# RMS weight moved into the PSUM eviction of the first two blocks, and a re-ordered start, in a fused sliding-window attention and SwiGLU kernel

## The chip, the cores and the metric

One core of one Trainium2 chip runs the whole program. The metric is the device time of one execution in microseconds, measured on the chip. A time is the median of several executions.

I write TensorE, VectorE, ScalarE and GpSimd for what the profile calls PE, DVE, ACT and POOL. PEld is TensorE's loading of weights, which overlaps its matmuls. SP is the queue that issues the stores.

## The reference

```python
def _attn_ref(q, k, v, n_sink, window):          # 4 batches, 8 heads, 768 positions, 64 wide
    scores = 1/sqrt(D) * q @ k^T
    keep = (key position < n_sink) | (0 <= query - key < window)     # n_sink 4, window 128
    a = softmax(where(keep, scores, -1e9))
    return a @ v

def _moe_ref(x, w_gate, w_val, w_out, rms_g):    # 3072 tokens, 512 wide, 1536 inner
    xn = x / sqrt(mean(x*x) + 1e-6) * rms_g
    g = xn @ w_gate
    return (g * sigmoid(g) * (xn @ w_val)) @ w_out
```

The attention output, with heads side by side, is the x of the second part.

## The kernel before

The 3072 tokens are 24 blocks of 128. Four blocks make a group of 512 tokens for the feed-forward part. A prologue runs the attention of blocks 0 and 1. Then the feed-forward matmuls of group 0 start on those two blocks (`fa`), while blocks 2 and 3 are still in attention. From there on, units of attention ("slots") are woven between parts of the feed-forward matmuls.

The unit names recur below. `unit_t1` and `unit_t` transpose q and k of a block. `unit_bias`, `unit_sp` and `unit_s` make scores and exponentials. `unit_av` multiplies by v. `unit_rms` and `unit_xr` normalise. `unit_x` transposes the normalised block, so that it can be the moving operand of the gate and val matmuls.

The normalisation multiplies by the weight `gb` on VectorE, and ScalarE copies the transposed block out of PSUM:

```python
    def unit_xr(g):
        ...
            nc.vector.scalar_tensor_tensor(
                out=XR[g][-1], in0=x16[:, c], scalar=y[:, 4:5], in1=gb[:, c],
                op0=ALU.mult, op1=ALU.mult,
            )
    def unit_x(g):
        ...
            nc.scalar.copy(
                out=XNT[G][:, c.start // P:c.stop // P, tb * P:(tb + 1) * P],
                in_=ps[:, 0:n].rearrange("p (k c) -> p k c", c=P),
            )
```

The end of the prologue, and the slots of group 0 (cut):

```python
        unit_warm(WARM[1])                   # filler matmuls
        unit_x(0)
        unit_t1(2, 0)
        unit_warm(WARM[2])
        unit_x(1)
        ...
        pools.close()                        # the prologue's PSUM pool ends here
    ...
        slots = [[lambda: unit_t1(5, 0)], [lambda: unit_t1(5, 1)], [lambda: unit_s(4)],
                 [lambda: unit_sink_scores(0, 4)], [lambda: unit_t(6)], []]
        for g in range(5, NB + 3):
            slots += step(g)
```

`weave` spreads the slots of a group evenly over its parts, so the number of slots decides which part comes ahead of which unit.

The softmax here doesn't subtract the row's maximum and nothing guards it: scores larger than these inputs give would overflow.

## Time and profile before

| | before |
|---|---|
| time, median of 3 executions | 255.21 us (254.88 to 255.5) |
| span of the profiled execution | 252.6 us |
| TensorE busy | 238.8 us, 95% |
| first gate matmul starts | 16.90 us |
| k of block 8 lands | 51.61 us |
| first gate matmul of group 1 | 73.35 us |

These are lines of the profile page. In the slices each digit is a busy share in tenths, and one slice is 6.3 us.

```profile
span 252.6 us, 4804 instructions
PE 238.8 (95%) x1733; PEld 127.4 (50%) x1760; DVE 181.1 (72%) x474; ACT 139.6 (55%) x312; POOL 98.1 (39%) x129
...
PE   5988979989999999999999999999999999999994
...
PEclk9999999999999999999999999999999999999999
DMA  9999999999999999650120550321321013200022
```

The lost time of TensorE is at the start. The view by windows says how much. Its columns are the window, its length, then the busy us of PE, PEld, DVE, ACT and POOL with the number of instructions, and last the granted clock, the DMA share and GB/s.

```profile
0.00:17.00 17.00, 12.50 (x102) 5.83 (x104) 11.00 (x46) 9.16 (x21) 15.70 (x26) 1.00 1.54 151
17.00:40.00 23.00, 20.47 (x234) 16.27 (x233) 16.39 (x43) 15.63 (x35) 17.63 (x22) 1.00 1.96 175
40.00:60.00 20.00, 18.51 (x199) 12.84 (x199) 17.76 (x50) 15.78 (x35) 13.82 (x17) 1.00 1.98 174
60.00:100.00 40.00, 39.68 (x309) 21.06 (x314) 35.52 (x100) 28.83 (x67) 27.49 (x33) 1.00 2.38 163
```

The waits of TensorE are in its timeline (start, duration, line, operation, count, and in brackets the idle time ahead of it with what ended it). L581 is the helper of the gate and val matmuls, L563 transposes a normalised block, L251 transposes q and k.

```profile
16.90 1.03 PE L581 MATMUL pg<-xnt,wg 128*128 128x256 bf16 x8 [0.46 <-ACT xnt L567]
...
50.68 0.40 PE L251 MATMUL pqk<-ident,qs 128*128 128x128 bf16 x4 [0.61 <-DMA qs<-in_q_dram]
51.65 0.40 PE L251 MATMUL pqk<-ident,ks 128*128 128x128 bf16 x4 [0.58 <-DMA ks<-in_k_dram]
51.89 1.03 PE L581 MATMUL pvl<-xnt,wv 128*128 128x512 bf16 x4
```

The last pair before 52 us are the transposes of block 8. They wait for its q and k. The chain of waits (start, duration, what) agrees: it reaches back from TensorE's work to this load.

```profile
39.14 12.47 DMA ks<-in_k_dram
51.61 0.04 issue
51.65 0.40 PE pqk L251 x4
52.05 0.86 PE pvl L581 x4
...
59.74 0.86 PE po L622 x4
60.60 0.44 PE pss L321 x4
```

The load was issued at 39.14 us and landed 12.47 us later, behind everything issued before it. From the transposes of block 8 to the first gate matmul of group 1 (51.65 to 73.35 us), the pieces of this chain add up to 15.87 us of TensorE, 4.16 of VectorE and 1.47 of ScalarE.

### The profile page before, as it was taken

The numbers are of one execution on the slowest core, as the hardware profiler recorded it, in microseconds if no ns is written. First come the engines' busy times: TensorE is split into PE (matmuls) and PEld (weight loads), VectorE is DVE, ScalarE is ACT, GpSimd is POOL, SyncE is SP. The second block draws the span as 40 slices with busy tenths as digits, with TensorE's granted clock in tenths as the row PEclk, the third lists the DMA queues.
The fourth block names the chain that finished last, engine by engine and source line by source line (L and its number), as shares of the span: only waits on it lengthen the run. The fifth ranks groups of instructions, "written<-read, shape, count | busy, mean of one in ns | idle before, by whom it ended". The sixth has DMA issues, their size and how long they took to land.

```text
span 252.6 us, 4804 instructions
## 1 busy us (share of the span) xinstructions
PE 238.8 (95%) x1733; PEld 127.4 (50%) x1760; DVE 181.1 (72%) x474; ACT 139.6 (55%) x312; POOL 98.1 (39%) x129
## 2 busy tenths in 40 slices
PE   5988979989999999999999999999999999999994
PEld 1446858655555454454454454454454544444441
DVE  5666869889779999539989459988359991287700
ACT  2757858879886465556473546466545441323211
POOL 8996779289985763134041004044201000000000
PEclk9999999999999999999999999999999999999999
DMA  9999999999999999650120550321321013200022
GB/s 130 152 174 189 189 156 188 182 155 150 194 186 161 155 131 155 128 168 13 21 56 10 145 145 3 64 58 19 113 84 23 0 21 98 91 0 0 0 86 83
DMA packets 105850, 25.74 MB, mean 102 GB/s; under 512 B 95074, under 2 KB 102754, under 8 KB 105827
## 3 DMA queue, kind: packets, MB, share of 16 engines
q0 software_dynamic: 80704, 13.90, 76.5%
q1 hardware_dynamic: 24082, 11.28, 18.6%
q10 hardware_dynamic: 1040, 0.26, 0.5%
q8 instruction: 14, 0.23, 0.4%
q14 instruction: 10, 0.07, 0.1%
HBM read 28.31 MB, written 6.29 MB: 137 GB/s over the span
## 4 chain that ended last, share of the span: by engine, by line
PE 67%; DMA 12%; DVE 8%; POOL 7%; ACT 2%; issue 2%; POOLq 0%; ACTq 0%; DVEq 0%
PE po L622 23%; PE pvl L581 18%; PE pg L581 18%; DMA wv<-in_moe_w_val_dram 7%; DMA ks<-in_k_dram 5%; PE pT L413 3%; DVE p L599 2%; POOL v L124 2%; POOL qs L111 2%; DVE hT L607 2%; PE pv L456 1%; PE pv L452 1%; PE pv L444 1%; POOL ks L111 1%; ACT et L422 1%
## 5 line engine op out<-in xcount | busy, mean ns | idle before, releaser
L581 PE MATMUL pg<-xnt,wg 128*128 128x512 bf16 (+1 forms) x317 | 73.5, 352 | 1.1 <-ACT xnt L567 0.5
L581 PE MATMUL pvl<-xnt,wv 128*128 128x512 bf16 (+1 forms) x322 | 73.4, 353 | 0.4
L622 PE MATMUL po<-wo,hT 128*128 128x512 bf16 x279 | 64.9, 379 | 0.5 <-issue 0.2
L594 ACT ACTIVATE th<-pg 128x512 bf16<-128x512 f32 x72 | 42.9, 596 | 39.1 <-PE pg L581 39.0
L599 DVE SCALAR_TENSOR_TENSOR p<-th,pg 128x512 bf16<-128x512 bf16 x72 | 48.9, 679 | 20.1 <-ACT th L594 19.5
L607 DVE TENSOR_TENSOR hT<-p,pvl 128x512 bf16<-128x512 bf16 x72 | 49.2, 684 | 3.7 <-PE pg L581 0.5
L581 PEld LDWEIGHTS <-wv 128*128 128x128 bf16 x328 | 30.5, 98 | 27.2 <-issue 1.1
L581 PEld LDWEIGHTS <-wg 128*128 128x128 bf16 x328 | 30.4, 98 | 26.9 <-issue 1.2
L422 ACT ACTIVATE et<-pT 128x512 bf16<-128x512 f32 x76 | 39.8, 602 | 4.8 <-PE pT L413 4.6
L390 POOL TENSOR_SCALAR_AFFINE_SELECT et<-et 128x512 bf16<-128x512 bf16 x20 | 13.1, 660 | 73.9 <-ACT et L422 73.9
L622 PEld LDWEIGHTS <-hT 128*128 128x128 bf16 x288 | 26.7, 98 | 29.7 <-issue 0.8
L494 ACT ACTIVATE sq<-x 128x256 bf16<-128x256 bf16 x48 | 20.0, 417 | 26.5 <-DVE x L484 26.1
L629 ACT ACTIVATE osb<-po 128x512 f32<-128x512 f32 x24 | 14.4, 602 | 25.9 <-PE po L622 20.8
L111 POOL DMA_DIRECT2D qs<-in_q_dram x23 | 20.7, 900 | 7.9 <-DMA wo<-in_moe_w_out_dram 2.2
L124 POOL DMA_DIRECT2D v<-in_v_dram x24 | 21.7, 903 | 4.4 <-DMA qs<-in_q_dram 2.6
L111 POOL DMA_DIRECT2D ks<-in_k_dram x23 | 20.6, 895 | 6.4 <-DMA wo<-in_moe_w_out_dram 3.2
L484 DVE TENSOR_TENSOR x<-pv,rden 128x256 bf16<-128x256 f32 x48 | 20.2, 421 | 0.8
L541 DVE SCALAR_TENSOR_TENSOR xr<-x,y,gb 128x512 bf16<-128x512 bf16 (+1 forms) x25 | 19.8, 795 | 0.7
L479 DVE RECIPROCAL rden<-pv 128x4 f32<-128x4 f32 x48 | 8.4, 175 | 16.1 <-PE pv L456 16.0
L388 DVE TENSOR_TENSOR et<-et,masks 128x1024 bf16<-128x1024 bf16 (+1 forms) x22 | 13.9, 638 | 3.5 <-ACT et L422 3.5
L456 PE MATMUL pv<-v,et 128*128 128x65 bf16 x168 | 15.3, 193 | 0.0
L452 PE MATMUL pv<-v,et 128*128 128x65 bf16 x136 | 12.7, 193 | 0.0
(75 smaller groups left out, 213.1 us busy)
## 6 DMA issues: line engine op xcount, KB each, us to landing
out_dram<-osb SPq DMA_DIRECT2D x24, 256.0 KB, 2.2
v<-in_v_dram POOLq DMA_DIRECT2D x24, 128.0 KB, 7.9
qs<-in_q_dram POOLq DMA_DIRECT2D x23, 128.0 KB, 8.2
ks<-in_k_dram POOLq DMA_DIRECT2D x23, 128.0 KB, 7.7
wg<-in_moe_w_gate_dram POOLq DMA_DIRECT2D x6, 256.0 KB, 7.6
wv<-in_moe_w_val_dram POOLq DMA_DIRECT2D x6, 256.0 KB, 8.2
wo<-in_moe_w_out_dram POOLq DMA_DIRECT2D x2, 768.0 KB, 10.6
osb<-in_k_dram ACTq DMA_DIRECT2D x1, 256.0 KB, 4.8
```

What stands on the lines that cost most here:

```text
L111: nc.gpsimd.dma_start(out=tl, in_=src[b, :, t * P:(t + 1) * P, :].rearrange("h t d -> t h d"),)
L124: nc.gpsimd.dma_start(out=V16[b][:, t, :, 0:D], in_=v[b, :, t * P:(t + 1) * P, :].rearrange("h t d -> t h d"),)
L422: nc.scalar.activation(out=et[:, hi].rearrange("p j n c -> p (j n c)"), in_=banks[u][hi], func=ACT.Exp, scale=inv_sqrt_d,)
L456: nc.tensor.matmul(out=dest, lhsT=E[(g, h, 0)], rhs=V16[b][:, t, h, :], start=(t == 0), stop=True, skip_group_check=True,)
L484: nc.vector.tensor_tensor(out=X16[g][:, heads_of(g, u), :], in0=pvv[:, :, 0:D], in1=RDEN.pop((g, u)).unsqueeze(2).to_broadcast((P, 4, D)), ...
L494: nc.scalar.activation(out=sq, in_=xh, func=ACT.Square, scale=MS_SCALE, accum_out=MS[g][:, u:u + 1],)
L541: nc.vector.scalar_tensor_tensor(out=XR[g][-1], in0=x16[:, c], scalar=y[:, 4:5], in1=gb[:, c], op0=ALU.mult, op1=ALU.mult,)
L581: nc.tensor.matmul(out=ps[:, i * n:(i + 1) * n], lhsT=w_sb[:, kt, ft * P:(ft + 1) * P], rhs=XNT[G][:, kt, cols], start=(kt == 0), stop=(kt ...
L594: nc.scalar.activation(out=st["th"], in_=st["pg"], func=ACT.Tanh, scale=0.5)
L599: nc.vector.scalar_tensor_tensor(out=p1, in0=st["th"], scalar=1.0, in1=st["pg"], op0=ALU.add, op1=ALU.mult,)
L607: nc.vector.tensor_tensor(out=HT[key][:, i:i + n, cols], in0=p1.rearrange("p (n c) -> p n c", n=n), in1=pvl.rearrange("p (n c) -> p n c", ...
L622: nc.tensor.matmul(out=st["po"], lhsT=HT[(G, ft // 2)][:, ft % 2, tb * P:(tb + 1) * P], rhs=wo[:, ft, :], start=(ft == 0), stop=(ft == FTN ...
```

## The change

The intent is to shorten the prologue. Blocks 0 and 1 are scaled by the RMS factor alone, and the weight is multiplied in when the transposed block leaves PSUM. There it is a per-partition scalar (`gt`), made by four tiny matmuls. Fillers go into more of TensorE's waits, so that its clock stays up. The k transposes of block 2 and the next-block scores of block 1 move from group 0 into the prologue. The slots of group 0 are re-ordered. Core of the diff, with cuts:

```diff
+    def unit_gt():
+        ps = pp[0].tile([P, 512], FP32, name="pgt", tag="ph", bufs=6)
+        for kt in range(KTN):
+            nc.tensor.matmul(
+                out=ps[:, kt:kt + 1], lhsT=raw[2][0:1, kt * P:(kt + 1) * P],
+                rhs=gb[0:1, 0:1], start=True, stop=True, skip_group_check=True,
+            )
+        nc.scalar.copy(out=gt, in_=ps[:, 0:KTN])
 ... unit_xr
+        if g < 2:
+            nc.vector.tensor_scalar(
+                out=XR[g], in0=x16, scalar1=y[:, 4:5], scalar2=None, op0=ALU.mult,
+            )
+            return
 ... unit_x
+            if g >= 2:
+                nc.scalar.copy(out=dest, in_=src)
+            elif k0 > 0:
+                nc.vector.tensor_tensor(out=dest, in0=src, in1=gt[...], op=ALU.mult)
+            else:
+                for i in range(n):
+                    nc.scalar.mul(dest[:, i, :], src[:, i, :], gt[:, k0 + i:k0 + i + 1])
 ... prologue
-        unit_warm(6)
+        unit_warm(9)
 ...
+        unit_gt()
+        pgb = unit_gb()
 ...
         unit_x(0)
         unit_t1(2, 0)
-        unit_warm(WARM[2])
+        unit_bias(1, 1)
+        unit_warm(1)
         unit_x(1)
+        unit_t1(2, 1)
+        unit_sp(1, 1)
+        nc.scalar.copy(out=gb, in_=pgb)
 ... group 0
-            [lambda: unit_t1(2, 1), lambda: unit_bias(1, 1), lambda: unit_sp(1, 1), lambda: unit_sink(0)],
-            [lambda: unit_t1(3, 0), lambda: unit_s(2)],
+            [lambda: unit_sink(0)],
+            [lambda: unit_t1(3, 0)],
+            [lambda: unit_s(2)],
 ...
-        slots = [[lambda: unit_t1(5, 0)], [lambda: unit_t1(5, 1)], ..., [lambda: unit_t(6)], []]
+        slots = [[], [lambda: unit_t1(4, 1)], [], [lambda: unit_t1(5, 0)], [lambda: unit_t1(5, 1)], ..., [lambda: unit_t(6)]]
```

More of the change, by code (lines that the diff above doesn't have):

```diff
@@ L91 @@
     PROLOGUE = [True]
-    WARM = (3, 4, 5, 2)
     QS, KS_, V16 = {}, {}, {}
@@ L99 @@
     gb = const.tile([P, DM], FP32, name="gb")
+    gt = const.tile([P, KTN], FP32, name="gt")
     idle = const.tile([P, 512], BF16, name="idle")
@@ L181, in unit_gb @@
         )
-        nc.scalar.copy(out=gb, in_=ps)
+        return ps
+    def unit_gt():
[6 more added lines that the diff above has]
+        nc.scalar.copy(out=gt, in_=ps[:, 0:KTN])
     with tc.manual_schedule(engines={mybir.EngineType.Pool, mybir.EngineType.DVE}):
@@ L433, in unit_s @@
                         E[(g, 2 * (u * per + j) + hi, n)] = et[:, hi, j, n, :]
-    def halves(g):
-        return [slice(0, DM // 2), slice(DM // 2, DM)] if g == 1 else [slice(0, DM)]
     def unit_av(g, u):
@@ L537, in unit_xr @@
         y, x16 = Y.pop(g), X16.pop(g)
-        XR[g] = []
-        for c in halves(g):
-            XR[g].append(xpool.tile([P, c.stop - c.start], BF16, name="xr", bufs=3))
-            nc.vector.scalar_tensor_tensor(
-                out=XR[g][-1], in0=x16[:, c], scalar=y[:, 4:5], in1=gb[:, c],
-                op0=ALU.mult, op1=ALU.mult,
-            )
+        XR[g] = xpool.tile([P, DM], BF16, name="xr", bufs=3)
+        if g < 2:
+            nc.vector.tensor_scalar(
+                out=XR[g], in0=x16, scalar1=y[:, 4:5], scalar2=None, op0=ALU.mult,
+            )
+            return
+        nc.vector.scalar_tensor_tensor(
+            out=XR[g], in0=x16, scalar=y[:, 4:5], in1=gb, op0=ALU.mult, op1=ALU.mult,
+        )
         if g >= DMA_X_FROM:
@@ L549, in unit_xr @@
             nc.sync.dma_start_transpose(
-                out=XNT[G][:, :, tb * P:(tb + 1) * P], in_=XR.pop(g)[0],
+                out=XNT[G][:, :, tb * P:(tb + 1) * P], in_=XR.pop(g),
             )
@@ L558, in unit_x @@
             XNT[G] = xtpool.tile([P, KTN, GN], BF16, name="xnt")
-        for xr, c in zip(XR.pop(g), halves(g)):
-            n = c.stop - c.start
+        xr = XR.pop(g)
+        n = KTN // 2 if g == 1 else KTN
+        for k0 in range(0, KTN, n):
             ps = pp[0].tile([P, 512], FP32, name="pxt", tag="b1").bitcast(BF16)
-            for i in range(n // P):
+            for i in range(n):
+                kt = k0 + i
                 nc.tensor.transpose(
-                    out=ps[:, i * P:(i + 1) * P], in_=xr[:, i * P:(i + 1) * P],
+                    out=ps[:, i * P:(i + 1) * P], in_=xr[:, kt * P:(kt + 1) * P],
                     identity=ident,
                 )
-            nc.scalar.copy(
-                out=XNT[G][:, c.start // P:c.stop // P, tb * P:(tb + 1) * P],
-                in_=ps[:, 0:n].rearrange("p (k c) -> p k c", c=P),
-            )
+            dest = XNT[G][:, k0:k0 + n, tb * P:(tb + 1) * P]
+            src = ps[:, 0:n * P].rearrange("p (k c) -> p k c", c=P)
+            if g >= 2:
+                nc.scalar.copy(out=dest, in_=src)
+            elif k0 > 0:
+                nc.vector.tensor_tensor(
+                    out=dest, in0=src,
+                    in1=gt[:, k0:k0 + n].unsqueeze(2).to_broadcast((P, n, P)),
+                    op=ALU.mult,
+                )
+            else:
+                for i in range(n):
+                    nc.scalar.mul(dest[:, i, :], src[:, i, :], gt[:, k0 + i:k0 + i + 1])
     HT = {}
@@ L683 @@
         unit_norm(0, 0, PV[(0, 0)])
+        unit_warm(2)
         unit_sp(1, 0)
@@ L688 @@
         unit_sq(0, 1)
-        unit_warm(WARM[0])
-        for u in range(2):
-            unit_av(1, u)
-            unit_norm(1, u, PV[(1, u)])
-            unit_sq(1, u)
-        unit_gb()
+        unit_warm(3)
+        unit_av(1, 0)
+        unit_norm(1, 0, PV[(1, 0)])
+        unit_sq(1, 0)
+        unit_warm(1)
+        unit_av(1, 1)
+        unit_norm(1, 1, PV[(1, 1)])
+        unit_sq(1, 1)
+        unit_gt()
+        pgb = unit_gb()
         unit_rms(0)
@@ L698 @@
         unit_xr(1)
-        unit_warm(WARM[1])
+        unit_warm(3)
         unit_x(0)
         unit_t1(2, 0)
-        unit_warm(WARM[2])
+        unit_bias(1, 1)
+        unit_warm(1)
         unit_x(1)
+        unit_t1(2, 1)
+        unit_sp(1, 1)
+        nc.scalar.copy(out=gb, in_=pgb)
         nc.vector.tensor_scalar(
@@ L723 @@
         weave(fa, [
-            [lambda: unit_t1(2, 1), lambda: unit_bias(1, 1), lambda: unit_sp(1, 1), lambda: unit_sink(0)],
-            [lambda: unit_t1(3, 0), lambda: unit_s(2)],
-            [lambda: unit_sink_scores(0, 2)],
-            [lambda: unit_t1(3, 1), lambda: unit_bias(3, 0), lambda: unit_av(2, 0), lambda: unit_sp(3, 0), lambda: unit_av(2, 1)],
+            [lambda: unit_sink(0)],
+            [lambda: unit_t1(3, 0)],
+            [lambda: unit_s(2)],
+            [lambda: unit_sink_scores(0, 2), lambda: unit_t1(3, 1)],
+            [lambda: unit_bias(3, 0), lambda: unit_av(2, 0), lambda: unit_sp(3, 0), lambda: unit_av(2, 1)],
             [lambda: unit_av(3, 0)],
-            [lambda: unit_av(3, 1), lambda: unit_t1(4, 0)],
-            [lambda: unit_bias(3, 1), lambda: unit_sp(3, 1)],
+            [lambda: unit_av(3, 1)],
             [lambda: unit_x(2)],
-            [lambda: unit_t1(4, 1)],
-            [lambda: unit_x(3)],
+            [lambda: unit_t1(4, 0)],
+            [lambda: unit_bias(3, 1), lambda: unit_x(3), lambda: unit_sp(3, 1)],
         ], first=True)
-        slots = [[lambda: unit_t1(5, 0)], [lambda: unit_t1(5, 1)], [lambda: unit_s(4)], [lambda: unit_sink_scores(0, 4)], [lambda: unit_t(6)], []]
+        slots = [[], [lambda: unit_t1(4, 1)], [], [lambda: unit_t1(5, 0)], [lambda: unit_t1(5, 1)], [lambda: unit_s(4)], [lambda: unit_sink_scores(0, 4)], [lambda: unit_t(6)]]
+        pre = len(slots)
         for g in range(5, NB + 3):
             slots += step(g)
-        slots[6].pop()
-        slots[10].pop()
+        slots[pre].pop()
+        slots[pre + 4].pop()
         outs = []
@@ L753 @@
                 outs = []
-            n1 = 6 + 4 * ((G + 2) * GB + 2 - 5) + 1
+            n1 = pre + 4 * ((G + 2) * GB + 2 - 5) + 1
             weave(parts, slots[n:n1], 1)
```

## The prediction

> **What bounds the kernel now.** TensorE is busy 95% of the span (page, part 1), and over 99% from 60 to 240 us (windows). What is lost is lost early: it is busy 12.50 of the first 17 us, 20.47 of 17 to 40, 18.51 of 40 to 60. The chain of waits says what sets that stretch: it runs along the load queue to the load of k of block 8, issued at 39.14 and landed at 51.61 us. TensorE's transposes of block 8 wait for it (timeline: idle 0.61 us for q at 50.68, 0.58 us for k at 51.65), and from there the chain is TensorE to the end. Until then the DMA engines are 90% busy in every slice, and loads land one behind another (q8 50.63, k8 51.61, v8 52.66, q9 53.48). No load before block 8 waits for TensorE or for a buffer; GpSimd waits only for earlier DMAs. The Trainium skill, "DMA: Bandwidth & Descriptors", section "Anatomy of one DMA", says the DMA engines wait for no semaphore and just consume their queues, which agrees with these landings. So k8 should land at about 51.6 us whatever the prologue does.
>
> **What the change does.** The RMS weight leaves the VectorE products (xr 0.75 and 2 x 0.44 us become plain scalings, estimated 0.42 each from the 512-wide copy) and goes into the PSUM evictions: for block 0, four ScalarE pieces of 128 columns (estimate 0.28 each, from 0.49 and 0.35 per 512 and 256 columns) instead of one copy of 0.59. The first gate matmul should start at about 16.4 instead of 16.9 us, with block 2's k transposes and block 1's second bias and scores (0.22 + 0.43 + 0.34 us) already done: about 1.5 us of head start. Fillers run in waits and cost nothing; no slice was throttled before, so nothing is won there.
> In the woven order block 5's transposes move two to three parts later, away from the waits before 35.11 and 35.95 us (0.72 + 0.45); with the head start TensorE should reach them near 33 us and wait for q5 again (landed 35.06).
> At block 8 all of this is lost: I estimate arrival near 48 to 49 us and a wait of 2 to 3 us, where it was 1.2. Only what moved across that wait survives: exactly one part, the val matmuls of f-tile 10 (4 x 512 columns, 0.86 us), now comes before block 8's transposes. From group 1 on the order is the same. Later loads (q9 53.48, used at 56; q10 56.16, used at 62) have slack for it.
>
> **Prediction.** 255.21 - 0.86, about 254.3 us; 253.4 to 255.0 in 8 of 10. Faster by over 2%: 3%; within 2%: 95%; slower: 2%.
>
> **What would show it.** First gate matmul 0.3 to 0.8 us earlier; a wait for q5 near 34 us; TensorE idle 2 to 3 us before 51.6; landings of q8 and k8 unchanged within 0.3 us; the span after k8's landing shorter by 0.8 to 0.9 us.
>
> **What would make it wrong.** If k8's landing moves, the end moves one for one. If the ScalarE pieces, the moved exps or the reuse of prologue PSUM banks delay the first gate matmul by over 3 us, it gets slower. If VectorE (17.76 of 20 us busy at 40 to 60) makes xr of blocks 4 and 5 late behind the wait, part of the 0.86 goes. If q8's wait does not bind, the head start shows, up to 3 us.

## More of the kernel before

The loads are issued by GpSimd in this order (first part cut):

```python
        for g in range(GB + 1, 2 * GB):      # blocks 5 to 7
            load_q(g)
            load_k(g)
            load_v(g)
        load_wo(0)
        last_load = load_wo(1)               # output weights, 2 x 768 KB
    with tc.issue_after(last_load):
        for g in range(2 * GB, NB):          # blocks 8 to 23
            load_q(g)
            load_k(g)
            load_v(g)
```

## The result, and the profile after

| | before | after |
|---|---|---|
| first measurement, medians of 4 executions | 255.26 us | 254.90 us (254.57 to 255.28) |
| ratio, 95% interval | | 0.9988 (0.9966 to 1.0009): same |
| repeated later with 5 rounds (run e10 below) | 254.74 us | 254.29 us (254.06 to 254.57) |
| ratio, 95% interval | | 0.9981 (0.9969 to 0.9993): 0.2 to 0.8 us faster |

Here and below a ratio compares the fast executions of one kernel with those of the kernel before that ran beside it, and it is not quite the ratio of the medians.

The page of the first profiled execution of the changed kernel (255.28 us, the slowest of the four):

```profile
span 253.6 us, 4855 instructions
PE 243.2 (96%) x1769; PEld 130.0 (51%) x1769; DVE 181.5 (72%) x474; ACT 139.4 (55%) x316; POOL 98.2 (39%) x129
...
PE   8979979999999999999999999999999999999994
...
PEclk9999988999999999999999999999999999999999
DMA  9999999999999999751011540320321002200022
```

The row of the clock has two slices below 9, which the kernel before had not. The windows show the same: more of the first 17 us is filled, and the mean clock from 17 to 40 us is 0.93.

```profile
0.00:17.00 17.00, 14.64 (x125) 7.83 (x126) 11.10 (x47) 9.67 (x26) 15.40 (x26) 1.00 1.48 149
17.00:40.00 23.00, 19.84 (x206) 15.86 (x206) 15.37 (x40) 13.10 (x31) 17.88 (x22) 0.93 1.97 175
40.00:60.00 20.00, 19.37 (x206) 13.45 (x203) 18.19 (x48) 16.48 (x34) 14.20 (x17) 1.00 1.98 174
```

TensorE's timeline of that execution (L600 is now the helper of gate and val, L573 the transposes of a normalised block):

```profile
17.95 1.03 PE L600 MATMUL pg<-xnt,wg 128*128 128x256 bf16 x8 [1.62 <-ACT gb L731]
...
34.22 0.40 PE L573 MATMUL pxt<-ident,xr 128*128 128x128 bf16 x4 [1.80 <-DVE xr L550]
...
35.29 1.24 PE L600 MATMUL pg<-xnt,wg 128*128 128x256 bf16 x8
36.32 1.92 PE L600 MATMUL pvl<-xnt,wv 128*128 128x256 bf16 x8
```

Three things are to be seen. The first gate matmul starts at 17.95 us and not at 16.4, after a wait of 1.62 us for ScalarE's copy of `gb` out of PSUM (e3 below shows what stands behind that copy). Block 3's transposes wait 1.80 us for VectorE's `xr`. Right after that wait, eight val matmuls take 1.92 us where they took 1.04 us before. The trace records a clock of one half from 35.97 us for 3.41 us; below I call that a throttled stretch. In this execution TensorE came to block 8 only after its k had landed (51.33 us), and did not wait for it.

The repeated measurement has an execution without such a stretch (254.19 us). It is the better one to hold against the prediction:

```profile
18.38 1.03 PE L600 MATMUL pg<-xnt,wg 128*128 128x256 bf16 x8 [1.62 <-ACT gb L731]
...
50.87 0.40 PE L260 MATMUL pqk<-ident,qs 128*128 128x128 bf16 x4
51.83 0.40 PE L260 MATMUL pqk<-ident,ks 128*128 128x128 bf16 x4 [0.57 <-DMA ks<-in_k_dram]
```

TensorE still waits for k of block 8 (landed at 51.78 us), but only 0.57 us, and hardly for q. Its chain of waits starts from the same load as before, and then looks different:

```profile
39.55 12.24 DMA ks<-in_k_dram
...
51.83 0.41 PE pqk L260 x4
...
52.27 1.01 ACT qkT L295
...
55.15 0.17 DVE m L509
...
56.49 0.60 DVE et L397
57.09 0.07 DVE y L531
57.16 0.60 DVE et L397
57.76 0.66 DVE xr L550
...
66.68 0.75 DVE xr L550
67.43 1.20 DVE et L397 x2
...
73.14 0.38 PE pg L600
```

From block 8's transposes to the first gate matmul of group 1 (51.83 to 73.14 us), its pieces add up to 0.41 us of TensorE, 11.52 of VectorE and 7.10 of ScalarE, the rest being issue. Before, most of it was TensorE. So the stretch behind the load has changed hands.

### The profile page after: what moved, and what is told of

Read it like the earlier page. It is cut to its first block, busy times and chain, and to the rows that moved or that the text cites. A ratio compares the mean times of both kernels' runs of the same rounds, so it can differ in the third digit from the quotient of the medians.

```text
span 253.6 us, 4855 instructions
## 1 busy us (share of the span) xinstructions
PE 243.2 (96%) x1769; PEld 130.0 (51%) x1769; DVE 181.5 (72%) x474; ACT 139.4 (55%) x316; POOL 98.2 (39%) x129
## 4 chain that ended last, share of the span: by engine, by line
PE 74%; DVE 13%; ACT 3%; issue 1%; ACTq 0%; DVEq 0%
PE pvl L600 22%; PE pg L600 22%; PE po L641 21%; PE pT L422 3%; DVE hT L626 2%; DVE et L397 2%; DVE xr L550 2%; DVE p L618 2%; PE pv L462 1%; PE pv L458 1%; ACT sq L500 1%; PE pqk L260 1%; DVE x L490 1%; PE pv L450 1%; PE pss L330 1%
## 5 line engine op out<-in xcount | busy, mean ns | idle before, releaser
L600 PE MATMUL pg<-xnt,wg 128*128 128x512 bf16 (+1 forms) x328 | 74.7, 356 | 1.8 <-ACT gb L731 1.6
L600 PE MATMUL pvl<-xnt,wv 128*128 128x512 bf16 (+1 forms) x328 | 74.9, 357 | 0.3 <-DVE hT L626 0.2
L641 PE MATMUL po<-wo,hT 128*128 128x512 bf16 x288 | 66.2, 379 | 0.4 <-ACT et L431 0.4
L600 PEld LDWEIGHTS <-wg 128*128 128x128 bf16 x328 | 30.7, 99 | 28.9 <-issue 2.8
L600 PEld LDWEIGHTS <-wv 128*128 128x128 bf16 x328 | 31.0, 99 | 27.4 <-issue 1.2
L124 POOL DMA_DIRECT2D v<-in_v_dram x24 | 21.5, 896 | 5.7 <-DMA qs<-in_q_dram 3.3
L550 DVE SCALAR_TENSOR_TENSOR xr<-x,y,gb 128x512 bf16<-128x512 bf16 x22 | 18.2, 826 | 0.5
```

Source lines behind the costliest of these rows:

```text
L124: nc.gpsimd.dma_start(out=V16[b][:, t, :, 0:D], in_=v[b, :, t * P:(t + 1) * P, :].rearrange("h t d -> t h d"),)
L550: nc.vector.scalar_tensor_tensor(out=XR[g], in0=x16, scalar=y[:, 4:5], in1=gb, op0=ALU.mult, op1=ALU.mult,)
L600: nc.tensor.matmul(out=ps[:, i * n:(i + 1) * n], lhsT=w_sb[:, kt, ft * P:(ft + 1) * P], rhs=XNT[G][:, kt, cols], start=(kt == 0), stop=(kt ...
L641: nc.tensor.matmul(out=st["po"], lhsT=HT[(G, ft // 2)][:, ft % 2, tb * P:(tb + 1) * P], rhs=wo[:, ft, :], start=(ft == 0), stop=(ft == FTN ...
```

## The experiments

Twelve kernels ran, each with 5 rounds beside the kernel before. The first four ran on one chip, the next four on a second, the last four on a third. Besides the time I read three moments from each trace: the landing of k of block 8 ("k8"), the first gate matmul of group 1 ("G1"), and the end. From G1 to the end it was 179.16 to 179.25 us in all fourteen profiled executions, the kernels before and after included. So the end is set at G1, and anything a kernel gains or loses shows ahead of it.

| kernel | ratio (95% interval) | k8 lands | k8 to G1 | block 8's transposes to G1 | block 5's `m` to G1 |
|---|---|---|---|---|---|
| before | 1 | 51.61 | 21.74 | 21.70 | 17.26 |
| after (first, throttled stretch) | 0.9988 (0.9966 to 1.0009) | 51.33 | 23.06 | 22.24 | 18.01 |
| e10, after again | 0.9981 (0.9969 to 0.9993) | 51.78 | 21.36 | 21.31 | 17.99 |
| e1, order alone | 1.0012 (0.9986 to 1.0039) | 52.44 | 21.65 | 21.61 | 18.00 |
| e2, prologue alone | 1.0014 (0.9984 to 1.0044) | 52.86 | 21.74 | 21.70 | 17.26 |
| e3, early copy | 1.0003 (0.9975 to 1.0031) | 52.53 | 21.31 | 21.26 | 18.00 |
| e8, fillers | 0.9986 (0.9962 to 1.0009) | 51.79 | 21.29 | 21.25 | 17.99 |
| e11, later prologue | 1.0022 (1.0006 to 1.0038) | 52.51 | 21.73 | 21.69 | 17.26 |
| e4, loads moved | 0.9986 (0.9957 to 1.0015) | 43.80 | | 22.41 | 17.26 |
| e7, early copy and loads | 0.9967 (0.9945 to 0.9989) | 43.92 | | 22.21 | 17.99 |
| e9, all | 0.9954 (0.9940 to 0.9968) | 43.87 | | 22.23 | 18.00 |

The spread of k8's landing, 51.28 to 52.86 us over the ten profiled executions whose load order is unchanged, is larger than the effects that I am after. The distance from k8 to G1 does not contain it. The landing does not differ by prologue either: its mean is 52.01 us in the five with the old one and 52.06 in the five with the new one. Block 8's transposes are counted from the weight load of k's first transpose.

`m` is the first VectorE instruction of block 5's RMS step, 55.15 us in e10. From its start to G1 it is 17.99 to 18.01 us in all seven kernels of the table with the part moved across the wait, and 17.26 in all four with the part behind it. The work is not quite the same: VectorE has eight mask products between the two in the first case (e1, e10, e9), seven in the second (before). So whatever the kernels with the moved part gain or lose against one another lies ahead of `m`.

### e1: one part moved across the wait, and nothing else

```diff
-        slots = [[lambda: unit_t1(5, 0)], [lambda: unit_t1(5, 1)], ...
+        slots = [[], [], [lambda: unit_t1(5, 0)], [lambda: unit_t1(5, 1)], ...
```

(The places of two later slots, which are dropped, and the bound of the first group's slots move along by two.)

> The kernel before, with its own prologue; only two empty slots are put ahead of group 0's woven slots, so that exactly one part (the val matmuls of f-tile 10, 0.86 us) moves ahead of block 8's transposes. Theory A (the load of k8 binds, and only work moved across its wait counts): 0.8 to 0.9 us faster than before, about 254.4; k8 lands at 51.3 to 51.7, TensorE still waits for it. Rival B (the head start of the prologue is what made the change faster): same time as before, within 0.2 us.

It measured 254.87 against 254.38 us, ratio 1.0012 (0.9986 to 1.0039). The 0.86 us (0.9966) lie outside the interval: the part alone is not worth them. The trace says why. k8 lands at 52.44 and TensorE waits for it, as theory A had it. But k8 to G1 is 21.65 us, only 0.09 shorter than before, though 0.86 us of TensorE's work has left that stretch. The chain of waits in it adds up to 11.54 us of VectorE, 5.89 of ScalarE and 1.98 of TensorE. So theory A holds for the wait and fails for what the moved part is worth. Block 5's `m` does start 3.65 us after the landing instead of 4.48, 0.83 less, but from there to G1 it takes 0.74 us longer.

This trace also showed something about the start. The same two opening bias matmuls that took 0.59 us in the kernel before take twice that here, though this prologue is unchanged:

```profile
5.47 1.06 PE L349 MATMUL ph<-amasks,ident 128*128 128x512 bf16 x2
...
6.75 1.06 PE L349 MATMUL ph<-amasks,ident 128*128 128x512 bf16 x2
```

The clock came up to full at 10.38 us in this execution and at 4.69 in the first profile of before. Its first gate matmul starts at 18.51 us instead of 16.90.

### e2: the new prologue, with the part left where it was

```diff
-        slots = [[], [lambda: unit_t1(4, 1)], [], [lambda: unit_t1(5, 0)], ...
+        slots = [[lambda: unit_t1(4, 1)], [lambda: unit_t1(5, 0)], ...
```

> The kernel after, with the two empty slots of group 0 taken out, so that the part stays behind block 8's transposes as in the kernel before; the whole new prologue stays. Theory A: no gain over before, 255.2 within 0.3 us when no throttled stretch falls in the run, up to 0.6 more when one does. Rival B: as fast as the kernel after, 254.6 without a throttled stretch.

It measured 254.99 against 254.38 us, ratio 1.0014 (0.9984 to 1.0044), as theory A expected. (Its 255.2 and rival B's 254.6 were levels of the first measurement, where the kernel before took 255.26; here that kernel took 254.38, and the two unthrottled executions of e2 average 254.33.) k8 to G1 is 21.74 us, exactly that of before. So the new prologue on its own buys nothing. Four of its six executions had a throttled stretch. In the profiled one it follows the wait ahead of the first gate matmul:

```profile
17.80 1.29 PE L600 MATMUL pg<-xnt,wg 128*128 128x256 bf16 x8 [1.62 <-ACT gb L731]
...
19.31 1.92 PE L600 MATMUL pvl<-xnt,wv 128*128 128x256 bf16 x8
```

### e3: the copy of the broadcast weight moved early

```diff
         pgb = unit_gb()
+        nc.scalar.copy(out=gb, in_=pgb)
         unit_rms(0)
 ...
         unit_sp(1, 1)
-        nc.scalar.copy(out=gb, in_=pgb)
```

> The kernel after, with ScalarE's copy of the broadcast weight out of PSUM moved from behind the moved exps to its idle time before block 0's evictions. Theory C (the first gate matmul waits for the PSUM bank that this copy frees): first gate matmul at 17.4 us or earlier instead of 17.95. Theory A on the end: no gain in runs without a throttled stretch (254.6 stays), as the head start is lost again at the wait for k8; fewer throttled runs are possible. Rival: the end moves with the first gate matmul, by 0.5 us or more.

It measured 254.69 against 254.38 us, ratio 1.0003 (0.9975 to 1.0031). Theory C is half right, and its number missed. The wait for the copy is gone, but another stands behind it. The first gate matmul starts at 17.93 us, 1.09 us after the last transposed block is in SBUF, where it was 1.56 in the first profile of after and in e10:

```profile
17.93 1.03 PE L600 MATMUL pg<-xnt,wg 128*128 128x256 bf16 x8 [1.14 <-ACT etp L381]
```

It now waits for the exponentials of the scores that were moved into the prologue. The transposed blocks were ready by 16.84 us, so this wait too fits a PSUM bank that has to be emptied first. That reading was argued from the order of the code and not tested. Here k8 to G1 is 21.31 us.

### e4: q and k of block 8 loaded ahead of the output weights, in the kernel before

```diff
+        load_q(2 * GB)
+        load_k(2 * GB)
         load_wo(0)
         last_load = load_wo(1)
```

(And block 8 left out of the later loop, except for its v.)

> The kernel before, with the loads of q and k of block 8 issued ahead of the two loads of the output weights. Theory A: q8 and k8 land near 43 and 44 us, the waits of 0.61 and 0.58 us at block 8's transposes are gone, and the end moves by as much: 254.0 to 254.3. wo lands near 51.6 us, before its first use at 56. Rival D (behind that wait TensorE is held by VectorE's products anyway): less than half of it, 254.7 or more.

It measured 254.10 against 254.38 us, ratio 0.9986 (0.9957 to 1.0015). The loads land at 43.40 and 43.80 us, TensorE no longer waits for them, and wo lands at 51.91. In the medians the time is 0.3 us better, less than theory A's 1 us and near rival D; the interval allows both. (The 254.10 does lie inside theory A's 254.0 to 254.3, but the kernel before is itself 0.9 us faster here than in the first measurement.) The stretch from block 8's transposes to G1 grew from 21.7 to 22.41 us, so most of what the wait gave up went into it. This execution had the late clock (full at 9.64 us), which makes its arrival later than it need be.

### e5 and e6: is it VectorE? The masks of blocks 7 to 10 taken out, without and with the moved part

Both give a wrong result. e5 is the kernel before, and e6 is e1, each with this:

```diff
     def mask(ev, b, t, nq):
+        if 7 <= b * NT + t <= 10:
+            return
```

> The kernel before, without VectorE's mask products of blocks 7 to 10 (wrong result on purpose), about 2 x 0.6 us of VectorE per block taken out of the stretch behind block 8's loads. Theory F (behind the landing of k8, VectorE's and ScalarE's chain is as long as TensorE's, so both bind): little gain alone, as TensorE's own work still fills the stretch: from the landing of k8 to the first gate matmul of group 1 21.4 to 21.8 us (21.74 in the kernel before). Rival G (VectorE alone binds there): 20.5 us or less.

> The one-part reordering (val matmuls of f-tile 10 ahead of block 8's transposes), also without the mask products of blocks 7 to 10. Theory F: with VectorE relieved the moved 0.86 us shows: k8's landing to the first gate matmul of group 1 20.7 to 21.1 us, against 21.65 with the masks, and 0.6 to 0.9 less than the kernel before without masks. Rival H (the moved part is worth nothing for another reason, for example PSUM banks): still within 0.3 us of the kernel before without masks.

e5 measured 255.16 against 255.09 us, ratio 1.0007 (0.9985 to 1.0030), with k8 to G1 at 21.99 us, 0.2 above theory F's range. Rival G falls: without the moved part, VectorE alone does not bind. e6 measured 254.16 us, ratio 0.9980 (0.9955 to 1.0005). That is 1.0 us below e5 in the medians, on the side of theory F, but the two intervals overlap. The profile of e6 missed my expectation. Block 8's transposes came at 51.74 us, 0.46 after k8 had landed, so k8 to G1 (22.05 us) says nothing there. From the transposes it is 21.59 us, not 20.8. In its chain everything behind 56.5 us is TensorE, and all ahead of it VectorE and ScalarE. By these distances and by the times the pair is inconclusive. The distance from block 5's `m` to G1 contains neither the landing nor the late arrival, and it does say something: 17.36 us in e6 against 18.00 in e1, which has the eight mask products that e6 lacks (e5: 17.58). So on that stretch VectorE's masks cost the moved version 0.64 us. e12 asks again with the loads out of the way.

### e7: early copy and early loads on top of the change

The edits of e3 and e4 together, on the kernel after.

> The kernel after, with the early copy of the broadcast weight and with the loads of q8 and k8 ahead of the output weights. Theory A (the wait for k8 eats the head start, and the landing carries its scatter into the time): no wait for q8 or k8, block 8's transposes near 50.4 instead of 52.5 us, and the time 0.5 to 1.2 us below the kernel before on the same chip. Rival (VectorE's chain from the prologue on binds, the wait for k8 is only its shadow): within 0.3 us of the kernel before.

It measured 253.98 against 255.09 us, ratio 0.9967 (0.9945 to 0.9989), 0.84 us faster by the ratio and inside the expectation. No wait for q8 or k8 is left. Block 8's transposes start at 50.84 us, somewhat later than the 50.4 that I had put down. The chain of waits from 42.2 us to G1 is now VectorE and ScalarE alone, but for the issue gaps.

### e8: fillers in the two waits of the changed kernel

```diff
         unit_sp(1, 1)
+        unit_warm(5)
         nc.scalar.copy(out=gb, in_=pgb)
 ...
-            [lambda: unit_bias(3, 1), lambda: unit_x(3), lambda: unit_sp(3, 1)],
+            [lambda: unit_bias(3, 1), lambda: unit_warm(7), lambda: unit_x(3), lambda: unit_sp(3, 1)],
```

(With the fillers' PSUM tile taken from the main pool once the prologue is over.)

> The kernel after, with five filler matmuls in the wait before the first gate matmul and seven in the wait before block 3's transposes (1.1 and 1.5 us of the waits of 1.6 and 1.8). Theory T (these two waits of TensorE make the clock drop to half for 3.4 us in about half of the executions of the new prologue, 9 of 16 so far against 3 of 23 with the old one): mean clock 0.997 or more in at least 5 of 6 executions, and the mean time of them that of the unthrottled executions of the kernel after, 254.2 to 254.6. Rival: the share of executions at 0.993 stays at about half.

It measured 254.21 against 255.09 us, ratio 0.9986 (0.9962 to 1.0009). Five of six executions had a mean clock of 0.998 or more, and their mean time is 254.30 us, as theory T expected. A mean of 0.993 is what one stretch of 3.41 us at half clock gives in 253 us. Counted over all rounds (and the first measurement of after; e11 apart), 0.993 or less came in:

| kernels | throttled executions |
|---|---|
| old prologue (before, e1, e4, e5, e6) | 9 of 58 |
| new prologue, its two waits open (after, e10, e2, e3, e7) | 11 of 27 |
| new prologue, waits filled (e8, e9, e12) | 1 of 16 |

Within the four kernels of the middle row that had both kinds, a throttled execution was slower on average by 0.6 (after), 1.0 (e2), 0.75 (e3) and 0.8 us (e7). The others differ more widely: e1's one throttled execution was 0.2 us faster than the rest, e6's 1.4 slower. The share is not stable: e10, the same kernel as after, had none in five.

The counts do not show that the fillers did it. The first measurement and the first chip had 9 of 16 with the open waits, against 3 of 23 with the old prologue; on the two later chips it was 2 of 11 against 6 of 35, and the filled kernels ran only there. The traces add a hint. Count windows of 3.41 us from the moment at which the clock came up: the half-clock stretches of after and e2 begin exactly 9 and 4 windows later. The windows just ahead of them had TensorE busy for 1.75 and 1.53 us, and the next lowest of all profiled executions (the last 30 us left aside), 1.79, 1.79, 1.80 and 1.83 us (after, e10, e3, e2), were not followed by half clock. With the waits filled no window was below 2.67 us (e8; e9 and e12 stay above 2.75). The stretch of e11, behind a window of 2.7 us, does not fit this.

### e9: everything together

The edits of e3, e4 and e8 (with four fillers ahead of the first gate matmul) on the kernel after.

> The kernel after with everything that looked useful: early copy of the broadcast weight, q8 and k8 loaded ahead of the output weights, four fillers before the first gate matmul and seven before block 3's transposes. Expected: no wait for q8 or k8; mean clock 0.997 or more in at least 5 of 6 executions; first gate matmul of group 1 near 73.0 us; 0.8 to 1.3 us under the kernel before on the same chip, and at or below the early copy with the moved loads alone (0.9967).

It measured 253.59 against 254.74 us, ratio 0.9954 (0.9940 to 0.9968): about 1.2 us faster than the kernel before, and 0.7 us below the kernel after in the medians of the same chip (254.29). All five executions had a clock of 0.999 or 1.000. G1 was at 72.70 us (expected near 73.0). This is the best correct kernel.

### e10: the changed kernel again

> The changed kernel itself once more, beside the others. Expected from the parts found so far: executions without a throttled stretch 0.4 to 0.7 us under the kernel before, throttled ones (0.993), two or three of six, at the time of the kernel before or above; together a ratio of 0.998 to 1.000. Had the 0.86 us of the prediction survived in full: 0.9966.

It measured 254.29 against 254.74 us, ratio 0.9981 (0.9969 to 0.9993), within what the parts had led me to expect, and with the full 0.86 us (0.9966) just outside the interval. No execution was throttled, where I had expected two or three.

### e11: the prologue made later on purpose

```diff
-    WARM = (3, 4, 5, 2)
+    WARM = (3, 4, 10, 2)
```

> The kernel before with five more filler matmuls ahead of block 1's transposes in the prologue, so that the first gate matmul starts about 1.1 us later. Theory A (the wait for q8 and k8 absorbs what the prologue loses or wins): the waits for q5, k5, q8 and k8 shrink by that much and the time stays within 0.3 us of the kernel before. Rival B (the start of the gate matmuls sets the time): 0.8 to 1.1 us slower, ratio 1.003 to 1.0045.

It measured 255.23 against 254.74 us, ratio 1.0022 (1.0006 to 1.0038). That is about 0.55 us slower, more than theory A's 0.3 and less than rival B's 0.8; the interval, 0.15 to 0.97 us, allows both. Three of six executions were throttled, which I had not expected of five fillers. In the profiled one a half-clock stretch lies on the fillers themselves, and the first gate matmul is 2.5 us later than in the first profile of before, at 19.38 us. Even so TensorE still came to block 8 ahead of its loads:

```profile
51.58 0.40 PE L251 MATMUL pqk<-ident,qs 128*128 128x128 bf16 x4 [0.16 <-DMA qs<-in_q_dram]
52.55 0.40 PE L251 MATMUL pqk<-ident,ks 128*128 128x128 bf16 x4 [0.57 <-DMA ks<-in_k_dram]
```

k8 to G1 is 21.73 us, as before. So in that execution the wait absorbed the whole delay. Why the times are 0.55 us higher all the same is open, and with it how far the wait absorbs a later start: the other executions have no landing times. The three unthrottled ones average 255.06 us.

### e12: e9 without the masks of blocks 5 to 8

Wrong, with the same edit as e5 but for blocks 5 to 8.

> The combined version without VectorE's mask products of blocks 5 to 8 (wrong result on purpose). Theory F (with the wait for k8 gone, VectorE's chain from 43 us on sets the pace): block 8's transposes to the first gate matmul of group 1 at most 21.6 us instead of 22.2, and 0.3 to 0.8 us faster than the combined version. Rival (TensorE alone sets it): no difference from the combined version.

It measured 252.74 us against 253.59 of e9 and 254.74 of before, ratio 0.9917 (0.9901 to 0.9933). The interval is clear of e9's. The windows from block 8's transposes to G1, first e9 and then e12, show what changed:

```profile
50.47:72.70 22.23, 21.05 (x204) 12.34 (x204) 18.53 (x61) 20.06 (x48) 19.61 (x23) 1.00 2.36 168
```

```profile
50.36:71.83 21.47, 20.61 (x204) 12.29 (x205) 16.19 (x55) 20.23 (x48) 18.39 (x21) 1.00 2.36 169
```

VectorE has 2.3 us less to do (third busy figure, 18.53 to 16.19), and the stretch is 0.76 us shorter, with the same matmuls. Theory F holds here: once TensorE no longer waits for the loads, VectorE's work, with ScalarE's in the same chain, holds it up. The gain lies ahead of block 5's `m` (54.70 us in e9, 53.82 in e12); from there to G1 it is 18.00 and 18.01 us. So e12 shows what VectorE costs ahead of `m`, and e6 what it costs behind. Of the 21.47 us that are left ScalarE is busy for 20.23 and TensorE for 20.61, so which would be next is open.

## Why the prediction was right or wrong

The time predicted, 254.3 us (253.4 to 255.0), holds the first measurement of 254.9 near its upper end, and the repeated one of 254.29. The class, within 2%, was right. The steps are less good than the sum, and that the number lies inside is partly luck: the range is 1.6 us wide, twice the gain that was forecast, and the two wrong arrival times lie ahead of the wait for block 8, which hides them while it lasts.

- **The load of block 8 bounds the start: right.** TensorE waits for k8 in before, e1, e2, e3, e5, e8, e10 and e11 (in the first profile of after and in e6 it came after the landing), and the changed prologue alone gives no gain (e2). The stated 51.6 us within 0.3 held for the first profile after (51.33), but ten executions spread from 51.28 to 52.86. The prediction took one landing for a constant.
- **"The first gate matmul should start at about 16.4 instead of 16.9 us ... about 1.5 us of head start": wrong.** It started at 17.95, and at 17.80 to 18.38 us in the other kernels with this prologue. The pieces were sized well: `xr` took 0.35 and 0.39 us (estimate 0.42; 0.82 and 0.41 in e10), the four ScalarE pieces 1.14 us together (estimate 4 x 0.28). What was missing is a wait for ScalarE: 1.62 us for its late copy of `gb`, and with that copy moved (e3) still 1.14 us for the moved exponentials. Both stood among the risks, as the moved exps and the reuse of prologue PSUM banks, and not in the sum. The start is also not a fixed number: with the old prologue it was 16.7 to 18.5 us from one execution to another, by when the clock came up.
- **"A wait for q5 near 34 us" and "arrival near 48 to 49 us and a wait of 2 to 3 us": wrong.** No wait for q5 occurred. The arrival was just under 51 us, with 0.57 us of wait for k8 left (e10). The head start had already gone into the wait of 1.62 us and the one of 1.80 us for block 3's `xr`, a VectorE chain that the estimate left out.
- **"Fillers run in waits and cost nothing; no slice was throttled before, so nothing is won there": wrong in its reason.** One unthrottled profile was taken as the rule. The old prologue had 9 throttled executions in 58, so it was throttled before too. The new one, with its two waits, had 11 in 27, but nine of these in the first measurement and on the first chip. A throttled one cost 0.6 to 1.0 us in these kernels. In the first measurement two of four were throttled, which takes about 0.3 us (half of 0.6) off its mean gain.
- **The 0.86 us that survive: the right mechanism, the wrong size.** The part did move across the wait, and k8 to G1 did get shorter: by 0.38 us in e10, 0.43 in e3 and 0.45 in e8. It is nothing in e2, where the part stays, and 0.09 in e1, which moves only the part. So the term measured about 0.4 us instead of 0.86. The repeated time agrees (0.9981 of 254.74 is 0.48 us less, with an interval of 0.2 to 0.8). The rest came back as waits for VectorE and ScalarE: their share of the chain in that stretch went from 5.6 to 18.6 of about 21.5 us, and with the masks out the stretch from block 5's `m` to G1 fell from 18.00 (e1) to 17.36 us (e6). Ahead of `m`, taking masks out of e9 gained 0.85 us in the medians (e12). This too stood among the risks ("part of the 0.86 goes"), but the sum assumed that TensorE alone filled the stretch. VectorE's 17.76 of 20 us, against TensorE's 18.51, should have said that it had little slack too.

Why the part is worth 0.4 us behind the new prologue but only 0.1 behind the old one is settled only as to the place. From block 5's `m` to G1 both take 18.00 us to within 0.01, filled by VectorE and ScalarE. The difference lies ahead of it: from k8's landing to `m` it is 3.65 us in e1, and 3.37, 3.31 and 3.30 in e10, e3 and e8. What shortens that piece was not tested.

## What to carry to other kernels

Find the wait that ends last and ask what lies on either side of it: work saved ahead of a wait for a load is lost as long as the wait is there (e2), and only work moved across it, or the load itself moved earlier, counts. Then check that the stretch behind it is not filled just as tightly by a second engine: here an engine that was 89% busy took back about half of what the first one saved. A gain of a few tenths of a microsecond should be read as a distance between two events of the trace rather than as a difference of whole times, when one load's landing alone scatters by more than a microsecond.

## What the Trainium skill lacked or had wrong

- "TensorE: Matmul & The Clock Gate", section "HAM oscillation — how this bites in real kernels", gives as the rule no idle gaps of TensorE beyond about 3.4 us. Here gaps half as long were followed by half clock. In the changed kernel one wait of 1.80 us, in a window of 3.41 us of which TensorE was busy 1.75 us, came just ahead of 3.41 us at half clock; in e2 it was a wait of 1.62 us (busy 1.53 of 3.41). The same 1.80 us wait did not throttle e10, where it lay in a window of 33.20 to 36.61 us with 1.96 us busy (windows counted as under e8, from the clock's coming up at 5.89 us). Part 1 of that page says that the window is free-running, which fits this. The length of 3.41 us is as the page states. In e11 a half-clock stretch followed a window in which TensorE was busy 2.71 of 3.41 us; why is not shown.
- The same page, Part 1, calls the ramp run-variable, and the runs agree. With six opening fillers the clock was full at 4.0 to 4.7 us in three profiled executions and at 9.6 to 10.4 us in three. With nine it was full by 6.8 us in all eight profiled ones.
- "DMA: Bandwidth & Descriptors", section "Anatomy of one DMA", gives about 2 us of fixed cost plus the bytes at 436 GB/s for a load from GpSimd. With the queue full, as here, k of block 8 took 12.47 us from issue to landing: what counts is what was issued before it, and putting it ahead of the output weights brought its landing from 51.6 to 43.8 us. No page gives the scatter of a landing deep in such a queue, 51.28 to 52.86 us here.
